# A Fourier stage folded four ways, with mirrored rows fetched and written by indirect DMAs

## The chip, the cores and the metric

The kernel runs on one core of a Trainium2 chip. The metric is the device time of one execution in microseconds. All arithmetic is in float32. The engines are named as in the profile: PE is TensorE (PEld its weight loads), DVE is VectorE, ACT is ScalarE, POOL is GpSimd, SP is SyncE, which here issues DMAs.

## The reference

Block attention with a decay is computed for four batches; its output, with the heads side by side, is a matrix x of 768 rows and 512 columns for each batch. x goes through the real part of a two-dimensional Fourier transform, is added to it, normalised by rows, and sent through a two-layer perceptron with a residual.

```python
def _moe_ref(x, w_ch1, w_ch2):              # x: (4, 768, 512)
    X = np.fft.fft(x, axis=1)               # along the 768 rows
    X = np.fft.fft(X, axis=2)               # along the 512 columns
    u = x + np.real(X).astype(np.float32)
    mu = np.mean(u, axis=-1, keepdims=True)
    var = np.mean((u - mu) ** 2, axis=-1, keepdims=True)
    un = (u - mu) / np.sqrt(var + 1e-06)
    ch = np.maximum(un @ w_ch1, 0.0) @ w_ch2   # 512 -> 2048 -> 512
    return (u + ch).astype(np.float32)
```

The attention before it, for a block of 64 rows, is a masked product of queries and keys times values, plus queries times a state, with powers of a factor `lam` per head; the state is then decayed and the block's keys and values are added to it. The two perceptron weights arrive as float64.

## The kernel before

A batch has six chunks of 128 rows. For each chunk `attn_chunk` loads keys, queries and values (SP queue, L210), transposes keys and queries (L221, L226), forms the scores of eight heads (L239), multiplies them by a decay table on VectorE (L243), updates the state (L254, L258, L259), applies state and scores (L267, L271), and transposes the result back (L278). ScalarE copies it into a tile x (L280). So the attention is done in chunks of 128 rows, not 64; the tables follow.

**The folds.** The Fourier transform of real rows needs cosines and sines only, and these are even and odd. So each chunk is folded along its columns, as soon as it is there, into sums and differences of columns d and 512-d (L288, L289 on VectorE, L287 on GpSimd for the two columns without a partner). Chunks 3 to 5 are then added to and subtracted from chunks 0 to 2 by GpSimd (L292, L293), which splits the rows' transform into even and odd frequencies (`fe`, `fo`).

**The Fourier stage** is the first part of `fft_ln`. L305 transforms along the rows, four column blocks and one single column, with tables `cs` of 193 frequencies, 30 matmuls in all; ScalarE copies the results (L313, L317) and VectorE makes a reversed copy (L320), because the frequencies above half are mirrored ones. L332 then transforms along the columns: six row tiles, four matmuls of 512 columns each, with the table `dt`. VectorE adds x (L335) and takes mean and variance (L337, L338); GpSimd forms the factor (L342, L343); VectorE normalises (L347), TensorE transposes (L351), ScalarE copies (L352).

**The perceptron**, `mlp`, works on pairs of row tiles: L363 for the first layer, relu alternately on VectorE (L369) and ScalarE (L371), L377 for the second. VectorE adds u (L382), SP stores the tile (L383). Both weights are converted from float64 on the chip, in 32 pieces of 512 columns, by VectorE and ScalarE (L181 to L189), each piece after its load (L176).

A float32 matmul is two rows in the profile, a transpose is one.

**The order.** The functions are generators that give an estimated duration after each piece, and `weave` interleaves two of them by a ratio:

```python
    run(weave(front(0), part(w, NW), 0.33))
    ...
            run(weave(part(fr, 44.0), weave(part(back, FO * 1.7 - 1.0), w, 0.9), 1.0))
            run(w)
            run(weave(fr, back, 1.0))
        elif b + 1 < B:
            run(weave(front(b + 1), back, 0.9 * t_mlp / t_front))
```

So batch 0's attention and Fourier stage run beside the first weight conversions; batch 1's beside the rest and batch 0's perceptron; batches 2 and 3 each beside the perceptron of the batch before; the last perceptron alone. From this order a scheduler makes the fixed instruction order of each engine; it can move an instruction past others by its own estimates, and each engine then runs in that order. Tiles come from pools: `xp` has twelve x tiles, `fp` one of each fold tile, `pa` five PSUM banks for the front, `pm` three for the perceptron.

Of the kernel before, what the change touches and what calls it, by code (L numbers as in the profile page):

```python
# [19 lines left out]
def _consts(S, DM):  # L20

    half, nk = S // 2, S // 4 + 1
    s = np.arange(half)
    k1 = np.stack([2 * np.arange(nk), 2 * np.arange(nk) + 1])
    ang = 2.0 * np.pi * ((s[:, None, None] * k1[None]) % S) / S

    cs = np.stack([np.cos(ang), np.sin(ang)]).reshape(2, half // 128, 128, 2, nk)
    cs = cs.transpose(2, 0, 1, 3, 4)

    h = DM // 2  # L30
    d = np.arange(h)
    k2 = np.arange(DM)
    ang = 2.0 * np.pi * ((d[:, None] * k2[None]) % DM) / DM

    dt = np.concatenate([np.cos(ang), -np.sin(ang)])
    dt[h] = np.where(k2 % 2 == 0, 1.0, -1.0)
    dt = dt.reshape(DM // 128, 128, DM).transpose(1, 0, 2)


    sgn = -np.ones((128, 1))  # L40
    sgn[0] = 1.0

    def c(m):
        return np.ascontiguousarray(m).astype(np.float32)

    return dict(cs=c(cs), dt=c(dt), sgn=c(sgn))
# [3 lines left out]
def kernel(  # L50
# [21 lines left out]
    HM = DM // 2  # L72
    G = 2
# [3 lines left out]
    cn = {n: nc.inline_tensor(a, name="k_" + n) for n, a in _consts(S, DM).items()}  # L77
# [4 lines left out]
    xp = ctx.enter_context(tc.tile_pool(name="xp", bufs=2 * NC))  # L82
# [22 lines left out]
    z = const.tile([H, 2 * C], F32, name="z")  # L105
# [26 lines left out]
    flip = fp.tile([128, 128], F32, tag="fb", name="flip")  # L132
# [19 lines left out]
    cs = const.tile([128, 2, HC, 2, NK], F32, name="cs")  # L152
    dt = const.tile([128, KO, DM], F32, name="dt")
    sgn = const.tile([128, 1], F32, name="sgn")
    w1 = const.tile([128, KO, DFF], F32, name="w1")
    w2 = const.tile([128, FO, DM], F32, name="w2")
    w1v = moe_w_ch1.rearrange("(c p) f -> p c f", p=128)
# [3 lines left out]
    def load_tables(i):  # L161
        if i == 1:
            nc.sync.dma_start(cs, cn["cs"].ap())
            nc.sync.dma_start(sgn, cn["sgn"].ap())
        elif i == 2:
            nc.sync.dma_start(dt, cn["dt"].ap())
# [34 lines left out]
    xs, folds = {}, {}  # L201
# [4 lines left out]
    def attn_chunk(b, c):  # L206
# [72 lines left out]
        x = xs[b, c] = new(xp, [C, DM], "x")  # L279
        nc.scalar.copy(x, px.rearrange("p h e -> p (h e)"))  # L280


        if c == 0:
            folds[b] = (new(fp, [C, HC, DM], "fe"), new(fp, [C, HC, DM], "fo"))
        fe, fo = folds[b]
        f = fo[:, c, :] if c < HC else new(fp, [C, DM], "fb")
        nc.gpsimd.tensor_copy(f[:, 0:DM:HM], x[:, 0:DM:HM])  # L287
        nc.vector.tensor_tensor(f[:, 1:HM], x[:, 1:HM], x[:, DM - 1:HM:-1], op=ALU.add)  # L288
        nc.vector.tensor_tensor(f[:, HM + 1:DM], x[:, 1:HM], x[:, DM - 1:HM:-1], op=ALU.subtract)  # L289
        if c >= HC:  # L290
            a = fo[:, c - HC, :]
            nc.gpsimd.tensor_tensor(fe[:, c - HC, :], a, f, op=ALU.add)  # L292
            nc.gpsimd.tensor_tensor(a, a, f, op=ALU.subtract)  # L293
        yield 1.7


    uts = {}

    def fft_ln(b):
        fe, fo = folds.pop(b)  # L300

        def dft_s(ps, cols, trig):
            for n, f in enumerate((fe, fo)):
                for t in range(HC):
                    nc.tensor.matmul(ps[:, n, :], lhsT=f[:, t, cols], rhs=cs[:, trig, t, n, :],  # L305
                                     start=(t == 0), stop=(t == HC - 1))

        ys = {}
        for c in (2, 3, 0, 1):
            ps = psum_a([128, 2, NK])  # L310
            dft_s(ps, slice(128 * c, 128 * c + 128), 0 if c < 2 else 1)
            y = new(fp, [128, NK, 2], f"y{c}")
            nc.scalar.copy(y, ps.rearrange("p n m -> p m n"))  # L313
            if c == 2:
                ps1 = psum_a([1, 2, NK])
                dft_s(ps1, slice(HM, HM + 1), 0)
                nc.scalar.copy(y[0:1], ps1.rearrange("p n m -> p m n"))  # L317
            yf = y.rearrange("p m n -> p (m n)")
            yr = new(fp, [128, S // 2], f"yr{c}")
            nc.vector.tensor_scalar(yr, yf[:, S // 2:0:-1],  # L320
                                    sgn if c == 2 else (1.0 if c < 2 else -1.0), None, op0=ALU.mult)
            ys[c] = (yf, yr)
            yield 4.0 if c == 2 else 2.0

        for g in range(NG):
            mv = new(np_, [128, G, 2], "mv")
            for i in range(G):
                T = G * g + i
                rev, tt = divmod(T, HC)
                ps = psum_a([128, DM])  # L330
                for c in range(KO):
                    nc.tensor.matmul(ps, lhsT=ys[c][rev][:, 128 * tt:128 * tt + 128], rhs=dt[:, c, :],  # L332
                                     start=(c == 0), stop=(c == KO - 1))
                u = xs[b, T]
                nc.vector.tensor_tensor(u, ps, u, op=ALU.add)  # L335
                stt = new(np_, [128, 6], "stt")
                nc.vector.bn_stats(stt, u)  # L337
                nc.vector.bn_aggr(mv[:, i, :], stt)  # L338
                yield 3.4
            ve = new(np_, [128, G], "ve")  # L340
            rs = new(np_, [128, G], "rs")
            nc.gpsimd.tensor_scalar(ve, mv[:, :, 1], EPS, None, op0=ALU.add)  # L342
            nc.gpsimd.tensor_tensor(rs, ve, mhalf, op=ALU.pow)  # L343
            ut = uts[b, g] = new(np_, [128, KO, G * 128], "ut")
            for i in range(G):
                un = new(np_, [128, DM], "un", bufs=1)
                nc.vector.tensor_scalar(un, xs[b, G * g + i], mv[:, i, 0:1], rs[:, i:i + 1],  # L347
                                        op0=ALU.subtract, op1=ALU.mult)
                pt = psum_a([128, KO, 128])
                for c in range(KO):  # L350
                    nc.tensor.transpose(pt[:, c, :], un[:, 128 * c:128 * c + 128], ident)  # L351
                nc.scalar.copy(ut[:, :, 128 * i:128 * i + 128], pt)  # L352
                yield 0.3


    def mlp(b):
        for g in range(NG):
# [15 lines left out]
            for i in range(G):  # L373
# [8 lines left out]
                nc.vector.tensor_tensor(u, ps, u, op=ALU.add)  # L382
                nc.sync.dma_start(out[b, 128 * T:128 * T + 128, :], u)  # L383
# [3 lines left out]
    def front(b):  # L387
        for c in range(NC):
            yield from attn_chunk(b, c)
        yield from fft_ln(b)  # L390
# [27 lines left out]
    run(weave(front(0), part(w, NW), 0.33))  # L418
    t_mlp = NG * (FO * 1.7 + G * 4 * 3.4)
    t_front = 66.0  # L420
    for b in range(B):
        back = mlp(b)
        if b == 0:
            fr = front(1)

            run(weave(part(fr, 44.0), weave(part(back, FO * 1.7 - 1.0), w, 0.9), 1.0))
            run(w)
            run(weave(fr, back, 1.0))
        elif b + 1 < B:
            run(weave(front(b + 1), back, 0.9 * t_mlp / t_front))  # L430
# [31 lines left out]
```

## Time and profile before

| | us |
|---|---|
| median of 3 runs (993.15 to 993.63) | 993.17 |
| the profiled execution | 996.47 |
| its span, first to last instruction | 994.5 |
| PE busy | 946.6 (95%) |
| DVE, ACT, POOL busy | 277.7, 174.9, 94.9 |
| L363 and L377, perceptron matmuls | 348.1 and 340.0 |
| L332, Fourier along columns | 44.7 + 43.0 |
| L305, Fourier along rows | 24.2 + 23.4 |
| PE idle up to the last L278 of batch 0, at 80.6 us | 32.3 |

The profiled execution is one run: durations of instructions come from it, and its span is 2.0 us shorter than its own time. In a row of the groups, the first numbers are tile names, shapes and count, then busy time and mean ns of one, then the engine's idle time ahead of it and what ended that. In a timeline a row is start, duration, engine, line and operation, with the idle time before it in brackets. Matmul rows overlap, so the step from one start to the next tells more of their cost than the duration. The clock is the share of full speed that TensorE was granted.

### The profile page before, as it was taken

The page shows a single profiled execution, that of the slowest core. Times are in us where ns is not written, and L with a number is a line of the kernel's source. Part 1 is how long each engine was busy: PE and PEld are TensorE (multiplying, and loading weights), DVE is VectorE, ACT ScalarE, POOL GpSimd, SP SyncE. Part 2 cuts the span into 40 slices and gives each one's busy share as a digit, 9 for nine tenths or more (in the row PEclk, how much of TensorE's full clock was granted, in tenths as well). Part 3 has the DMA queues.
Part 4 walks back from the last instruction along what each step waited for, and adds up shares of the span by engine and source line. Part 5 has one row for each costly group of instructions (what it writes and reads, how often), then busy time and mean ns, then how long its engine had stood idle before and what let it go on. Part 6 is the DMA issues. An engine that isn't in the chain of part 4 may idle for free.

```text
span 994.5 us, 10680 instructions
## 1 busy us (share of the span) xinstructions
PE 946.6 (95%) x4532; PEld 629.1 (63%) x4532; DVE 277.7 (28%) x546; ACT 174.9 (18%) x335; POOL 94.9 (10%) x117
## 2 busy tenths in 40 slices
PE   5569798999999999999999999999999999999998
PEld 3456476754756658568567558658657647566673
DVE  5787499522200012112102122212101212000010
ACT  4563266300000101111010002111101000000000
POOL 1223033400000001101200000011110000000000
PEclk9879999999999999999999999999999999999999
DMA  9963056300000011211100002120000000000000
GB/s 262 252 175 112 8 172 179 88 1 11 11 11 11 1 43 32 51 45 33 43 11 1 1 21 54 32 54 11 1 22 1 1 11 11 11 11 1 21 1 21
DMA packets 85039, 45.64 MB, mean 46 GB/s; under 512 B 76025, under 2 KB 77569, under 8 KB 84737
## 3 DMA queue, kind: packets, MB, share of 16 engines
q1 hardware_dynamic: 84992, 44.98, 16.5%
q8 instruction: 35, 0.57, 0.2%
q14 instruction: 12, 0.09, 0.0%
HBM read 38.67 MB, written 6.30 MB: 45 GB/s over the span
## 4 chain that ended last, share of the span: by engine, by line
PE 87%; DVE 5%; ACT 3%; POOL 1%; issue 1%; DMA 0%; POOLq 0%; DVEq 0%; ACTq 0%
PE pm L377 33%; PE pm L363 32%; PE pa L332 8%; PE pa L305 3%; PE pa L239 2%; PE pa L271 2%; PE pa L267 2%; PE pa L351 1%; PE pa L254 1%; PE pa L278 1%; ACT pw L182 1%; DVE pw L184 1%; PE pa L226 1%; PE pa L221 1%; DVE pw L181 1%
## 5 line engine op out<-in xcount | busy, mean ns | idle before, releaser
L363 PE MATMUL pm<-ut,w 128*128 128x256 f32 x1536 | 348.1, 382 | 1.2 <-ACT hr L371 1.2
L377 PE MATMUL pm<-w,hr 128*128 128x512 f32 x768 | 340.0, 594 | 0.0
L363 PEld LDWEIGHTS pm<-ut,w 128*128 128x128 f32 x1536 | 286.9, 190 | 48.1 <-issue 9.1
L377 PEld LDWEIGHTS pm<-w,hr 128*128 128x128 f32 x768 | 143.3, 190 | 165.4 <-issue 164.5
L371 ACT ACTIVATE hr<-pm 128x256 f32<-128x256 f32 x96 | 36.9, 384 | 427.2 <-PE pm L363 426.1
L369 DVE TENSOR_SCALAR hr<-pm 128x256 f32<-128x256 f32 x96 | 40.7, 424 | 238.9 <-PE pm L363 238.7
L382 DVE TENSOR_TENSOR x<-pm,x 128x512 f32<-128x512 f32 x24 | 16.6, 691 | 159.3 <-PE pm L377 159.0
L217 POOL TENSOR_TENSOR kd<-k,decay 128x512 f32<-128x512 f32 x20 | 22.5, 1126 | 254.4 <-PE pa L254 148.4
L335 DVE TENSOR_TENSOR x<-pa,x 128x512 f32<-128x512 f32 x24 | 16.6, 691 | 107.5 <-PE pa L332 107.5
L239 PE MATMUL pa<-qT,kT 64*128 64x128 f32 x384 | 32.4, 316 | 13.6 <-ACT qT L228 13.6
L332 PE MATMUL pa<-dt,y 128*128 128x512 f32 x96 | 44.7, 611 | 0.0
L239 PEld LDWEIGHTS pa<-qT,kT 64*128 64x128 f32 x384 | 27.3, 215 | 25.0 <-ACT qT L228 18.5
L332 PE MATMUL pa<-dt,yr 128*128 128x512 f32 x96 | 43.0, 592 | 0.0
L243 DVE TENSOR_TENSOR sc<-pa,decay 128x512 f32<-128x512 f32 x48 | 31.0, 685 | 22.1 <-PE pa L239 20.4
L271 PE MATMUL pa<-sc,v 128*64 128x128 f32 x384 | 30.3, 294 | 3.4 <-DVE sc L243 3.4
L332 PEld LDWEIGHTS pa<-dt,yr 128*128 128x128 f32 x96 | 17.9, 190 | 21.0 <-issue 21.0
L332 PEld LDWEIGHTS pa<-dt,y 128*128 128x128 f32 x96 | 18.3, 197 | 19.6 <-issue 18.3
L342 POOL TENSOR_SCALAR ve<-mv 128x2 f32<-128x2 f32 x12 | 3.0, 249 | 285.8 <-DVE mv L338 285.8
L271 PEld LDWEIGHTS pa<-sc,v 128*64 128x64 f32 x384 | 23.4, 146 | 9.7 <-DVE sc L243 4.6
L274 ACT COPY oT<-pa 128x512 f32<-128x512 f32 x24 | 14.0, 584 | 82.5 <-PE pa L271 82.5
L182 ACT ACTIVATE pw<-pw,cvt 128x512 uint16<-128x512 uint16 x32 | 22.9, 720 | 21.1 <-DVE pw L181 20.9
L223 ACT COPY kT<-pa 128x512 f32<-128x512 f32 x24 | 14.0, 584 | 69.8 <-PE pa L221 69.7
(65 smaller groups left out, 627.7 us busy)
## 6 DMA issues: line engine op xcount, KB each, us to landing
raw<-in_moe_w_ch_dram SPq DMA_DIRECT2D x32, 512.0 KB, 4.0
k<-in_k_dram SPq DMA_DIRECT2D x24, 256.0 KB, 3.2
q<-in_q_dram SPq DMA_DIRECT2D x24, 256.0 KB, 3.9
v<-in_v_dram SPq DMA_DIRECT2D x24, 256.0 KB, 3.0
out_dram<-x SPq DMA_DIRECT2D x24, 256.0 KB, 2.0
cs<-k_cs SPq DMA_DIRECT2D x1, 1158.0 KB, 6.4
dt<-k_dt SPq DMA_DIRECT2D x1, 1024.0 KB, 6.9
shifted<-zd SPq DMA_DIRECT2D x1, 512.0 KB, 5.7
```

The lines of the kernel that those rows point to most:

```text
L182: nc.scalar.activation(pw, pw, AF.Relu, bias=cvt[:, 0:1], scale=-1.0)
L217: nc.gpsimd.tensor_tensor(kd, kt, kpow, op=ALU.mult)
L239: mm(pss[hi][:, hp, :], lhsT=kT[HD[hi], hp, :], rhs=qT[HD[hi], hp, :], start=True, stop=True)
L243: nc.vector.tensor_tensor(t, pss[hi], decay[:, hi::2, :], op=ALU.mult)
L267: mm(po[HD[hi], hp, :], lhsT=s_old[HD[hi], hp, :], rhs=qs[HD[hi], hp, :], start=(hp == 0), stop=False, skip_group_check=True)
L271: mm(po[HD[hi], hp, :], lhsT=vt[:, 2 * hp + hi, :], rhs=sc[hi][:, hp, :], start=(c == 0 and hp == 0), stop=(hp == HP - 1), skip_group_chec ...
L305: nc.tensor.matmul(ps[:, n, :], lhsT=f[:, t, cols], rhs=cs[:, trig, t, n, :], start=(t == 0), stop=(t == HC - 1))
L332: nc.tensor.matmul(ps, lhsT=ys[c][rev][:, 128 * tt:128 * tt + 128], rhs=dt[:, c, :], start=(c == 0), stop=(c == KO - 1))
L363: nc.tensor.matmul(ps, lhsT=w1[:, c, 128 * fc:128 * fc + 128], rhs=ut[:, c, :], start=(c == 0), stop=(c == KO - 1))
L369: nc.vector.tensor_scalar(t, ps, 0.0, None, op0=ALU.max)
L371: nc.scalar.activation(t, ps, AF.Relu)
L377: nc.tensor.matmul(ps, lhsT=hr[fc // 4][:, fc % 4, 128 * i:128 * i + 128], rhs=w2[:, fc, :], start=(fc == 0), stop=(fc == FO - 1))
```

## The change

The Fourier stage now uses a second symmetry along each axis. The rows are folded as four quarters: row p goes with rows 384-p, 384+p and 768-p, and the columns likewise with 256-d and so on. The mirrored rows lie in other partitions, so each chunk of x is also stored in a DRAM tile (L320, on the ACT queue), and once all six are there five indirect DMAs on the POOL queue gather them reversed (`mirror`, L339 and L342). `fold` then makes the folded tiles for two row blocks, of 128 and of 65 rows, even parts on VectorE (L358, L359, L362, L368, L369, L375, L376) and odd parts on GpSimd (L360, L361, L364, L371, L372, L378, L379). It replaces the fold of each chunk as it comes.

L395 transforms along the rows with 20 matmuls of 193 columns. `width` transforms along the columns (L406 to L411): five matmuls of 128 or 129 columns for each of three row tiles, and three for a single row. Only half of the outputs are computed: a sum and a difference (L429, L430) give row k and its mirror 768-k, added to x on VectorE (L432) and to the gathered x on GpSimd (L433). L439 to L442 set the one row that is its own mirror. Row tiles 3 to 5 hold mirrored rows and columns; the columns are put right at the normalisation (L461) and at the output (L497, L498), the rows by an indirect DMA that scatters them to their places (L502, POOL queue) in place of a plain store by SP.

The order changes too. Batch 0's attention is woven with 12 weight pieces. Batch 0's Fourier stage then has half of batch 1's attention and four pieces beside it, and the perceptron of batch 0 starts beside the other half. The pool `xp` has ten tiles, and three more are in a new pool `xn`; the tables `cs` and `dt` are smaller, a table `ix` holds row numbers, and the five transformed tiles `ys` are fixed, zeroed once by GpSimd.

The core of the diff:

```diff
+        nc.scalar.copy(x[:, 0:HM], px[:, 0:HM])
+        nc.scalar.copy(x[:, HM:DM], px[:, DM - 1:HM - 1:-1])
...
+        nc.scalar.dma_start(xd[b][rows], x)
-        nc.vector.tensor_tensor(f[:, 1:HM], x[:, 1:HM], x[:, DM - 1:HM:-1], op=ALU.add)
-        nc.vector.tensor_tensor(f[:, HM + 1:DM], x[:, 1:HM], x[:, DM - 1:HM:-1], op=ALU.subtract)
-        if c >= HC:
-            a = fo[:, c - HC, :]
-            nc.gpsimd.tensor_tensor(fe[:, c - HC, :], a, f, op=ALU.add)
-            nc.gpsimd.tensor_tensor(a, a, f, op=ALU.subtract)
...
+    def mirror(b):
+        d = xd[b]
+        gather = nc.gpsimd.indirect_dma_start
+        r1 = [new(fp, [128, DM], f"r{a}") for a in range(2)]
+        for a, n in enumerate(BLK):
+            gather(out=r1[a][0:n], out_offset=None, in_=d[:, :], in_offset=row_of(a, n))
+        for t in range(HC):
+            u = xs[b, HC + t] = new(xp, [128, DM], "x")
+            gather(out=u[:, :], out_offset=None, in_=d[:, :], in_offset=row_of(2 + t))
...
+    def fold(b, r1):
+        for a, n in enumerate(BLK):
+            x0, x2, x3 = xs[b, a][0:n], xn_[b, HC + a][0:n], xs[b, HC + a][0:n]
+            x1 = r1[a][0:n]
...
+            V.tensor_tensor(e[0:n, 0, 0:DM], x0, x3, op=ALU.add)
+            V.tensor_tensor(e[0:n, 1, 0:DM], x1, x2, op=ALU.add)
+            P.tensor_tensor(o[0:n, 0, 0:DM], x0, x3, op=ALU.subtract)
+            P.tensor_tensor(o[0:n, 1, 0:DM], x1, x2, op=ALU.subtract)
+            V.tensor_tensor(e[0:n, :, 1:HM], e[0:n, :, 1:HM], e[0:n, :, HM:DM - 1], op=ALU.add)
+            P.tensor_tensor(o[0:n, :, 1:HM], o[0:n, :, 1:HM], o[0:n, :, HM:DM - 1], op=ALU.subtract)
...
+            V.tensor_tensor(am[:, 0, 0:HM + 1], lo, hi, op=ALU.add)
+            V.tensor_tensor(am[:, 1, 0:HM + 1], lo, hi, op=ALU.subtract)
+            P.tensor_tensor(bm[:, 0, 1:HM], lo, hi, op=ALU.subtract)
+            P.tensor_tensor(bm[:, 1, 1:HM], lo, hi, op=ALU.add)
...
+            V.tensor_tensor(f[0:n, 0], lo, hi, op=ALU.add)
+            V.tensor_tensor(f[0:n, 1], lo, hi, op=ALU.subtract)
+            P.tensor_tensor(f[0:n, 2], lo, hi, op=ALU.subtract)
+            P.tensor_tensor(f[0:n, 3], lo, hi, op=ALU.add)
...
+        for i in range(5):
+            for n in range(2):
+                for a, rows in enumerate(BLK):
+                    nc.tensor.matmul(ps[0:m, n, :], lhsT=f, rhs=cs[0:rows, a, i in (2, 3), n, :],
+                                     start=(a == 0), stop=(a == 1))
...
+        def width(t, ps, only_a):
+            mm(ps[:, HM + QM:DM], lhsT=y[2], rhs=dt[:, 2, 0:QM], start=True, stop=True)
+            mm(ps[:, HM:HM + QM + 1], lhsT=y[0], rhs=dt[:, 0, :], start=True, stop=False)
+            mm(ps[:, HM:HM + QM + 1], lhsT=y[4], rhs=dt[:, 4, :], start=False, stop=True)
+            mm(ps[:, 0:QM], lhsT=y[1], rhs=dt[:, 1, 0:QM], start=True, stop=True)
+            mm(ps[:, QM:HM], lhsT=y[3], rhs=dt[:, 3, 0:QM], start=True, stop=True)
...
+            nc.vector.tensor_tensor(even_odd(ds[:, 0:HM]), A, even_odd(B[:, :]), op=ALU.subtract)
+            nc.vector.tensor_tensor(even_odd(ds[:, HM + 1:2 * HM + 1]), A, even_odd(B[:, :]), op=ALU.add)
+            nc.vector.tensor_tensor(halves(u), halves(u), halves(ds)[:, :, 0:HM], op=ALU.add)
+            nc.gpsimd.tensor_tensor(halves(v_), halves(v_), halves(ds[:, 1:DM + 1])[:, ::-1, :], op=ALU.add)
...
-                for c in range(KO):
-                    nc.tensor.matmul(ps, lhsT=ys[c][rev][:, 128 * tt:128 * tt + 128], rhs=dt[:, c, :],
-                                     start=(c == 0), stop=(c == KO - 1))
...
+                if T < HC:
+                    nc.sync.dma_start(out[b, 128 * T:128 * T + 128, :], y)
+                else:
+                    nc.gpsimd.indirect_dma_start(out=out.rearrange("b s d -> (b s) d"),
+                                                 out_offset=row_of(2 + HC * (b + 1) + T - HC),
+                                                 in_=y[:, :], in_offset=None)
...
-    run(weave(front(0), part(w, NW), 0.33))
+    run(weave(attn(0), part(w, 0.75 * NW), 0.75 * NW / t_att))
+    fr = front(1)
+    run(weave(fft_ln(0), weave(part(fr, 0.5 * t_att), part(w, 0.25 * NW), 0.5 * NW / t_att), 1.5))
```

## The prediction

> **What bounds the kernel now.** I read the busy shares first, then the slices, the chain of waits, the costliest groups, and at last windows and timelines of single stages.
>
> ```profile
> PE 946.6 (95%) x4532; PEld 629.1 (63%) x4532; DVE 277.7 (28%) x546; ACT 174.9 (18%) x335; POOL 94.9 (10%) x117
> ...
> PE   5569798999999999999999999999999999999998
> ...
> PEclk9879999999999999999999999999999999999999
> ...
> PE 87%; DVE 5%; ACT 3%; POOL 1%; issue 1%; DMA 0%; POOLq 0%; DVEq 0%; ACTq 0%
> ...
> L332 PE MATMUL pa<-dt,y 128*128 128x512 f32 x96 | 44.7, 611 | 0.0
> ...
> L332 PE MATMUL pa<-dt,yr 128*128 128x512 f32 x96 | 43.0, 592 | 0.0
> ```
>
> TensorE is busy 95% of the span, and its idle time lies in the first eight slices; after that every matmul that is dropped is time gained, if nothing makes TensorE wait. Here is TensorE by stages (us, busy and rows, clock, DMA share, GB/s); the cuts are the last L278 of batch 0, its first L332, its last L351, and batch 1's last L278:
>
> ```profile
> 0.00:80.60 80.60, 48.26 (x424) 0.85 0.80 217
> 80.60:93.00 12.40, 11.52 (x65) 1.00 0.64 191
> 93.00:133.20 40.20, 34.52 (x114) 0.96 0.12 40
> 133.20:187.40 54.20, 50.40 (x463) 1.00 0.57 157
> 187.40:199.40 12.00, 11.22 (x85) 1.00 0.38 84
> 199.40:994.50 795.10, 790.63 (x3390) 1.00 0.07 18
> ```
>
> From 133.2 on, 852.2 us are busy and 9.1 idle (3.6 of them the tail): 133.2 + 852.2 + 9.1 = 994.5. Batch 2's turn from attention to Fourier shows how the present folds hide (timeline of TensorE):
>
> ```profile
> 719.22 0.60 PE L278 MATMUL pa<-ident,oT 128*128 128x128 f32 x4
> 719.66 7.03 PE L377 MATMUL pm<-w,hr 128*128 128x512 f32 x16
> 726.52 1.14 PE L305 MATMUL pa<-cs,fe 128*128 128x193 f32 x6
> ```
>
> Copy, fold and GpSimd adds fit under 6.87 us of L377. The last view is the one that the forecast hangs on, VectorE and GpSimd side by side:
>
> ```profile
> 83.68 0.68 DVE L184 SCALAR_TENSOR_TENSOR pw<-raw,pw 128x512 uint16<-128x512 uint16 x1
> 83.91 1.58 POOL L292 TENSOR_TENSOR fe<-fo,fb 128x512 f32<-128x512 f32 x1 [1.03 <-DVE fb L289]
> 84.28 1.48 DVE L181 TENSOR_SCALAR pw<-raw 128x512 uint16<-128x512 uint16 x1
> ...
> 85.56 1.33 POOL L293 TENSOR_TENSOR fo<-fo,fb 128x512 f32<-128x512 f32 x1
> 85.69 1.75 DVE L189 SCALAR_TENSOR_TENSOR w<-w,pw 128x512 f32<-128x512 f32 x1
> ```
>
> L181 usually takes 0.42 and L189 0.68; each here ends only when the GpSimd add ends, and L292 (1.27 at least) grows to 1.58. They take turns.
>
> **What the Trainium skill says.** "SBUF — State Buffer", Who interferes with whom: a VectorE instruction with two SBUF inputs and a GpSimd instruction that reads SBUF exclude each other for the whole instruction; the lines above agree. "GPSIMD Engine Reference", 4.1 Engine selection: two-input elementwise work is about 2x slower there; the trace agrees (128x512: 1.27 against 0.69). "TensorE: Matmul & The Clock Gate", What's actually happening: after an idle window of some 3.4 us TensorE runs at half clock, and some 3.4 us of work restore it; agrees: four L221 take 0.86 at 23.95 and 0.44 when busy. "DMA: Bandwidth & Descriptors", Anatomy of one DMA: a DMA issued by GpSimd takes 2.0 us plus bytes/436e3, 2.6 for 256 KB; Latency: about 1 us of it until the first byte. No run here shows one.
>
> **The change part by part.**
>
> *Removed from TensorE.* The width stage (L332) has 24 matmuls of 512 columns a batch, 21.6 us; now 15 of 128 or 129 columns and three one-row ones. L305 starts an instruction of 193 columns each 0.163 us, so 128 columns take 0.108; L278's 128x128 step is 0.11 (719.22 to 719.66 for four), so loading does not bind. Two instructions a matmul: 18 x 0.22 = 4.0. If loads of 190 ns (PEld rows of L332) did not overlap: 18 x 0.38 = 6.8. I take 4.0. The sequence stage (L305) falls from 30 matmuls to 20, 0.327 each: 9.8 to 6.5. Together 20.9 us a batch, **84 in all** (72 with the dear price).
>
> *Added ahead of the first Fourier matmul, in each batch.* The last chunk's x is copied in two pieces (ACT, two of about 0.38), stored to DRAM (2.0, as the outputs land), fetched mirrored by five gathers on POOL, and folded by 14 VectorE and 14 GpSimd instructions over two row blocks (65 rows cost as much as 128). VectorE: per block three of 0.60 and four of 0.34 (L188's and L289's starts), 3.2. GpSimd: three of 1.27 and four of 0.64 (L292; L258's 0.62), 6.4. By the turns shown above these add: 2 x 9.6 = 19.2. A gather's hold on POOL is between 1.0 (first byte) and 2.6 (whole transfer, one after another); I take 1.3, the lower end plus the 0.3 by which L292 is stretched, and 1.8 while weight conversion fills VectorE. All these gathers, and a 1.3 us scatter of the output, stand in POOL's in-order queue before or between the folds.
>
> *Batches 2 and 3.* From the last transpose: copies until 1.4, store landed and seen 3.6, five gathers until 10.1, the third landed 9.5. Taking turns, VectorE has the even half of block 0 at 14.8 (9.5 + 2.6 of folds + 2.7 of GpSimd's turns), GpSimd the odd half at 19.8 (10.1 + 6.4 + scatter 1.3 + 2 of VectorE's), that of block 1 at 27.6 (10.1 + 12.8 + 1.3 + 3.4). TensorE's built order there is 16 L377 (6.9), 9 MLP-up matmuls (3.9), two even Fourier ones, one odd, two MLP-up, then block 1: it waits 3.6, 4.3 and 6.6 us, 14.5, and 1.5 for the clock: **16 a batch, 32**. Bounds: 13 (gather 1.0), 23 (2.6).
>
> *Batch 1.* POOL issues three gathers; the fourth waits for a buffer (`xp` has 10) until output tile 0 of batch 0 is added, the fifth for tile 1. First wait: conversion shares VectorE and ACT (stored 5.5, third gather 10.9, landed 12.7; folds 2.6, conversion 1.3, turns 4.8), even data at 21.4, cover 20 MLP-up matmuls (9.1): 12.3. Second: tile 0 added, gather 1.3 + landing 1.8, 4.5 of odd folds plus turns of 2.5, about 11, against 7 L377 (6.0): 5. Then 3 in small waits up to the normalised transposes, 2 for the clock: **22** (15 to 31). Before, this stretch (187.4 on) idled 0.8.
>
> *Batch 0.* Of 13 weight conversions ahead of the last scores 10 are left in the built order, and the folds of 0.68 a chunk go: 3 x 2.5 + 4 = 11 us of VectorE, of which I count two thirds: last L278 at 73 for 80.6 (67 to 79). Store landed 5.5 after, five gathers of 1.8 until 14.5, GpSimd's folds 12.8 with 7 of VectorE's turns until 34, the last odd matmuls and chunk 0 of batch 1 until 40 (93.0 - 80.6 = 12.4 before). Then widths, normalisation and chunks 1 and 2: 17 of VectorE rows in a chain (adds and `bn_stats` of 0.60, quarters of 0.34) and some 10 of hand-overs: 27.5. Last transposes at 73 + 40 + 27.5 = **140.5** (129 to 153), with 15.2 us of batch 1's attention done (5.1 a chunk, 5.1 us being its warm rows in the chain) and 5.6 less of L363.
>
> *The other edits.* Copies in halves, `un` in halves, `y` in halves, the x0 fix-ups: VectorE and ACT gain under 5 us a batch, under MLP matmuls that leave VectorE 80% idle. Stores (1.5 MB) and gathers replace 1.4 MB of smaller tables in the loaded first 75 us: nothing. Last scatter instead of L383: 1.4 more at the tail.
>
> *The sum.* 140.5, plus TensorE's rest 852.2 - 15.2 + 5.6 - 3 x 20.9 = 779.9, plus waits: attention of batch 1 beside conversion 5 (5.3 before), batch 1 22, batches 2 and 3 32, tail 5. Total 984.4 us of span against 994.5: **10 us less**. The profiled execution took 996.47 in all, 3.3 above the median of 993.17; the same difference from the median gives **983**.
>
> **Rivals.**
> (a) *More of the gain stays.* Gathers of 1.0 and folds that overlap freely: batch 0 -10, batch 1 -5, the others -5 each, 25 less: 958. For it: POOL is busy 10%. Against: the turns at 84 us.
> (b) *The POOL queue becomes the bound; slower.* Gathers and scatters at 2.6: batch 0 +4 (5 x 0.8), batch 1 +4, batches 2 and 3 six each by 1.3, +16: 24 more, 1007. It decides where a hold is about 0.5 us over my prices, since 20 of them stand on the path and 10 us are to be lost. For it: L258 took 3.82 us once and a two-element L287 4.06 in dense VectorE stretches, six times normal. Against: their medians stay at 0.62 and 0.44.
> (c) *Everything is hidden:* 993 - 84 = 909. Against: the order above puts at most 12 us of matmuls over 27 of chain. The order also shows that the matmuls do go, so "nothing changes" is only a balance of gain and waits, 991 to 995.
>
> **How the numbers follow.** Forecast (965 to 991) 0.42; (a) with (c) 0.18; balance 0.10; (b) 0.30. A difference under 0.2%, 2 us, is about what a measurement of this kernel can tell from none. Signs are mixed; the likeliest case alone spans 965 to 991, and the range of 953 to 1010 leaves 0.2 outside, with (c) and the far end of (b). Faster 0.60, same 0.10, slower 0.30.
>
> **What would show it.** TensorE busy near 865 us; L406 to L411 together near 16 us. Waits of L395 on POOL and DVE folds of 11 to 20 us in each later batch, and clock digits under 9 there. Gathers and scatters as POOL work of 1.3 us; GpSimd folds stretched beside VectorE's. Batch 0's last L465 near 140. It is wrong if L395 waits little (then 950), if TensorE's small matmuls cost their loads (12 more), or if POOL's holds exceed 1.8 us.

## The result and the profile after

The changed kernel takes 1003.25 us (median of 4 runs, 999.76 to 1007.08), the one before on the same chip 993.16: a ratio of 1.0105, 95% interval 1.0059 to 1.0152. **It is slower by 1%.** The forecast was 983 and faster. The profiled execution took 1007.08, its span is 1005.3. It is the slowest of the four: they differ by 7 us, and their granted clocks with them (0.937, 0.940, 0.947, 0.947).

From the page of the changed kernel, the lines that answer to those of before: busy shares, slices, granted clock, chain.

```profile
PE 892.6 (89%) x4404; PEld 616.0 (61%) x4404; DVE 323.7 (32%) x610; ACT 186.1 (19%) x411; POOL 165.7 (16%) x176
...
PE   4642989598899999999986999999986999999997
...
PEclk9985799786999999999996999999995999999999
...
PE 73%; POOL 6%; DVE 6%; issue 3%; DMA 3%; ACT 1%; POOLq 0%; ACTq 0%
```

TensorE's busy time fell by 54.0 us, its idle time (span less busy) rose from 47.9 to 112.7. The clock, 0.986 of full speed over the span before, is 0.937. Its low digits stand beside or just after the idle ones: in batch 0's Fourier stage (slices 3 to 5), in batch 1's (8 to 10), in batch 2's (22) and in batch 3's (31). POOL and DVE, 1% and 5% of the chain before, now have 6% each.

By stages (us, busy and count for PE, PEld, DVE, ACT, POOL, then clock, DMA share, GB/s). The cuts: the last L313 of batch 0, its first L395, its last L465, batch 1's last L313, batch 1's last L465.

```profile
0.00:64.90 64.90, 38.33 (x428) 28.90 (x428) 52.39 (x101) 38.28 (x68) 13.99 (x26) 1.00 0.97 254
64.90:92.06 27.16, 0.11 (x2) 0.03 (x1) 18.97 (x22) 6.82 (x13) 16.65 (x15) 0.58 0.40 108
92.06:144.90 52.84, 45.02 (x336) 37.21 (x336) 31.19 (x61) 16.66 (x42) 19.88 (x20) 0.76 0.36 102
144.90:182.00 37.10, 32.09 (x272) 25.53 (x272) 34.89 (x71) 26.05 (x46) 3.12 (x3) 0.95 0.71 199
182.00:270.50 88.50, 69.88 (x229) 44.64 (x228) 45.05 (x81) 18.22 (x43) 30.04 (x28) 0.81 0.13 43
270.50:1005.30 734.80, 707.19 (x3144) 479.70 (x3144) 141.17 (x278) 80.05 (x200) 82.05 (x85) 0.97 0.09 27
```

Batch 0's Fourier stage begins with 27 us in which TensorE does nothing, and goes on at a clock of 0.76; batch 1's (182 to 270.5) has 18.6 us of idle and a clock of 0.81. Before, the last 795 us of the run went at 1.00.

Batch 2's turn from attention to Fourier, where the kernel before went from L377 straight into L305 (timeline of TensorE, changed kernel):

```profile
512.97 0.60 PE L313 MATMUL pa<-ident,oT 128*128 128x128 f32 x4
513.41 7.03 PE L491 MATMUL pm<-w,hr 128*128 128x512 f32 x16
520.28 4.05 PE L477 MATMUL pm<-ut,w 128*128 128x256 f32 x18
530.71 2.52 PE L395 MATMUL pa<-cs,fs 128*128 128x193 f32 x6 [6.39 <-DVE fs L375]
533.03 1.91 PE L477 MATMUL pm<-ut,w 128*128 128x256 f32 x4
539.76 2.30 PE L395 MATMUL pa<-cs,fs 65*128 65x193 f32 x6 [4.82 <-POOL fs L378]
```

Two waits, 6.4 and 4.8 us, in brackets. What the reader should see beside them is the work between and after: four L477 rows take 1.91, while 18 at full clock took 4.05. They run at half speed. VectorE and GpSimd in the same stretch (timeline of these two):

```profile
523.04 3.42 DVE L358 TENSOR_TENSOR fe<-x,x 128x512 f32<-128x512 f32 x1 [1.06 <-DMA x<-xd,ix]
523.40 1.28 POOL L361 TENSOR_TENSOR fo<-r,xn 128x512 f32<-128x512 f32 x1
524.63 1.27 POOL L360 TENSOR_TENSOR fo<-x,x 128x512 f32<-128x512 f32 x1
...
527.37 1.27 POOL L364 TENSOR_TENSOR fo<-fo 128x510 f32<-128x510 f32 x1
527.44 1.49 DVE L368 TENSOR_TENSOR fe<-fe 128x257 f32<-128x257 f32 x1 [0.26 <-ACT fe L363]
```

L358, which needs 0.60, holds VectorE for 3.42: it ends only when two GpSimd folds are through.

### The profile page after: what moved, and what is told of

The parts are those of the page before. It is cut to its first block, busy times and chain, and to the rows that moved or that the text cites. A ratio compares the mean times of both kernels' runs of the same rounds, so it can differ in the third digit from the quotient of the medians.

```text
span 1005.3 us, 10721 instructions
## 1 busy us (share of the span) xinstructions
PE 892.6 (89%) x4404; PEld 616.0 (61%) x4404; DVE 323.7 (32%) x610; ACT 186.1 (19%) x411; POOL 165.7 (16%) x176
## 3 DMA queue, kind: packets, MB, share of 16 engines
q1 hardware_dynamic: 83264, 40.73, 15.5%
## 4 chain that ended last, share of the span: by engine, by line
PE 73%; POOL 6%; DVE 6%; issue 3%; DMA 3%; ACT 1%; POOLq 0%; ACTq 0%
PE pm L477 30%; PE pm L491 29%; PE pa L395 4%; PE pa L306 2%; PE pa L274 2%; DMA x<-xd,ix 1%; PE pa L302 1%; PE pa L465 1%; PE pa L313 1%; PE pa L289 1%; POOL fo L360 1%; POOL fo L364 1%; POOL r L339 1%; DVE pw L219 1%; PE pa L261 1%
## 5 line engine op out<-in xcount | busy, mean ns | idle before, releaser
L477 PE MATMUL pm<-ut,w 128*128 128x256 f32 x1536 | 356.9, 389 | 1.7 <-DVE hr L483 0.7
L477 PEld LDWEIGHTS pm<-ut,w 128*128 128x128 f32 x1536 | 293.3, 194 | 47.7 <-issue 5.4
L395 PE MATMUL pa<-cs,fs 65*128 65x193 f32 (+1 forms) x128 | 42.7, 509 | 63.8 <-DVE fs L375 49.6
L497 DVE TENSOR_TENSOR y<-pm,x 128x256 f32<-128x256 f32 x24 | 10.2, 424 | 218.6 <-PE pm L491 218.6
L395 PEld LDWEIGHTS pa<-cs,fs 65*128 65x128 f32 (+1 forms) x128 | 36.2, 309 | 70.1 <-issue 39.4
L502 POOL DMA_INDIRECT out_dram<-y,ix x12 | 12.5, 1043 | 325.2 <-DVE y L498 324.9
L274 PE MATMUL pa<-qT,kT 64*128 64x128 f32 x384 | 30.5, 298 | 11.4 <-ACT qT L263 11.4
L278 DVE TENSOR_TENSOR sc<-pa,decay 128x512 f32<-128x512 f32 x48 | 31.3, 684 | 22.0 <-PE pa L274 20.3
L266 DVE TENSOR_TENSOR qs<-pa,qpow 128x512 f32<-128x512 f32 x20 | 13.8, 689 | 64.5 <-ACT qT L263 64.5
L433 POOL TENSOR_TENSOR x<-x,ds 128x512 f32<-128x512 f32 x12 | 18.2, 1515 | 77.3 <-DVE ds L430 70.4
L339 POOL DMA_INDIRECT r<-xd,ix x8 | 8.6, 1079 | 129.4 <-DMA xd<-xn 128.2
```

What stands on the lines that cost most here:

```text
L274: mm(pss[hi][:, hp, :], lhsT=kT[HD[hi], hp, :], rhs=qT[HD[hi], hp, :], start=True, stop=True)
L278: nc.vector.tensor_tensor(t, pss[hi], decay[:, hi::2, :], op=ALU.mult)
L339: gather(out=r1[a][0:n], out_offset=None, in_=d[:, :], in_offset=row_of(a, n))
L395: nc.tensor.matmul(ps[0:m, n, :], lhsT=f, rhs=cs[0:rows, a, i in (2, 3), n, :], start=(a == 0), stop=(a == 1))
L433: nc.gpsimd.tensor_tensor(halves(v_), halves(v_), halves(ds[:, 1:DM + 1])[:, ::-1, :], op=ALU.add)
L477: nc.tensor.matmul(ps, lhsT=w1[:, c, 128 * fc:128 * fc + 128], rhs=ut[:, c, :], start=(c == 0), stop=(c == KO - 1))
```

## The experiments

Theory W: waits for the chain of store, gathers and folds, with the half clock after them, take more than the matmuls give. Rivals: M, the many small matmuls cost more than the few wide ones; P, the turns of VectorE and GpSimd; Q, the queue of gathers; O, the new order of batches 0 and 1. Each kernel was timed beside executions of the kernel before; the ratio to these, with its interval, is what compares. Span, busy, idle and clock are TensorE's in the profiled execution, which lies between 3 us below and 9 us above its median (run 2 is the one at 9), so small differences between these columns tell nothing.

| kernel | median us | ratio (95%) | span | busy | idle | clock | waits of the row matmuls (L395) |
|---|---|---|---|---|---|---|---|
| before | 993.16 | 1 | 994.5 | 946.6 | 47.9 | 0.986 | 1.7 (L305) |
| changed | 1003.25 | 1.0105 (1.0059 to 1.0152) | 1005.3 | 892.6 | 112.7 | 0.937 | 63.7 |
| 1 cover in batches 2, 3 | 968.45 | 0.9735 (0.9695 to 0.9775) | 964.3 | 875.7 | 88.6 | 0.958 | 40.7 |
| 2 cover in all batches | 969.29 | 0.972 (0.9677 to 0.9763) | 977.0 | 889.8 | 87.2 | 0.949 | 14.0 |
| 3 no folds | 907.93 | 0.9111 (0.9076 to 0.9146) | 905.4 | 856.2 | 49.2 | 0.998 | none |
| 4 all folds on VectorE | 950.0 | 0.9543 (0.9508 to 0.9578) | 945.4 | 867.8 | 77.6 | 0.977 | 26.0 |
| 5 three gathers early | 990.3 | 0.9957 (0.9943 to 0.9971) | 986.8 | 886.0 | 100.8 | 0.953 | 49.2 |
| 6 order as before | 1015.1 | 1.0227 (1.0194 to 1.0259) | 1011.7 | 896.9 | 114.8 | 0.930 | 59.3 |
| 7 VectorE, gathers early | 941.51 | 0.9489 (0.9458 to 0.952) | 937.0 | 869.1 | 67.9 | 0.975 | 17.8 |
| 8 as 7, order as before | 955.84 | 0.9638 (0.9602 to 0.9674) | 952.4 | 877.3 | 75.1 | 0.963 | 20.2 |
| 9 short cover, idle wait | 996.86 | 1.0015 (0.9993 to 1.0038) | 997.4 | 890.4 | 107.0 | 0.945 | 59.0 |
| 10 wait filled, folds held | 1013.29 | 1.02 (1.0148 to 1.0253) | 1010.4 | 912.1 | 98.3 | 0.941 | 49.2 |
| 11 as 7, chunk ahead in batch 0 | 943.34 | 0.9482 (0.944 to 0.9525) | 940.2 | 872.0 | 68.2 | 0.971 | 7.8 |
| 12 wait filled | 993.89 | 1.0007 (0.9992 to 1.0023) | 991.2 | 899.9 | 91.3 | 0.964 | 41.5 |

**1, cover in batches 2 and 3.**

```diff
         sets = fold(b, r1)
+        if b >= 2:
+            yield 13.0
...
-    t_att, t_front = NC * 7.3, NC * 7.3 + 17.0
+    t_att, t_front = NC * 7.3, NC * 7.3 + 30.0
```

> In batches 2 and 3 the lead generator reports 13 units of its time after the folds, so that 28 MLP-down and 8 MLP-up matmuls (about 27 us) stand between the last attention transpose and the first Fourier matmul, where 8 and 9 (about 11 us) stood. Theory W (waits for the store-gather-fold chain, and the half clock after them, eat the gain): batch 2 has 11.2 us of idle and about 4 us of half clock, batch 3 10.5 and about 7; nearly all of it goes, 1003 becomes 970 to 980. Theory M (the many small matmuls cost more than the few wide ones did, whatever stands before them): no change, 1000 to 1006. Theory P (GpSimd and VectorE turns stretch every stage): 995 to 1003, since the folds are the same.

3.7% below the changed kernel (0.9735/1.0105), two lines of scheduling and nothing else. Busy falls by 16.9 with the same 4404 matmul rows, idle by 24.1. The two waits of each of these batches, 21.7 us, are gone, and with them their half clock, 11.2 us (how it is counted stands under run 3); the small rest lies in batches 0 and 1, which the edit leaves alone. That is W's number, even a little under it; neither M nor P, as the whole explanation, allows for it.

**2, cover in all batches.** The report is 13 units, 36 in batch 1.

> The same cover in all four batches: in batch 0 two and a half chunks of batch 1's attention are put ahead of the first Fourier matmul, in batch 1 the report is 36 units. Theory W: beyond the run with cover in batches 2 and 3 alone, batch 0 (27 us idle, about 10 us of half clock) gives 10 to 20 us and batch 1 (15 us idle, about 10 of half clock) 5 to 15, so 940 to 965. Theory O (the order of batch 1's attention beside batch 0's folds is itself the cost): batch 0 gives nothing, 965 to 980. Theory M: 1000 to 1006.

Nothing beyond run 1: the intervals overlap almost wholly. In batch 0 the wait moves (timeline of TensorE, run 2):

```profile
97.06 1.97 PE L302 MATMUL pa<-qs,st 64*64 64x128 f32 x16 [8.78 <-DVE qs L266]
...
138.18 1.09 PE L466 MATMUL pa<-ident,un 128*128 128x128 f32 x4 [8.13 <-DVE un L462]
```

The attention put ahead needs VectorE for qs and masks, where the folds and the weight conversion stand; later the normalised tiles are late (L466 there is the kernel's L465). By these waits VectorE's work, not the order of TensorE, is the limit of this stage; run 11 tries it once more. In batch 1 a wait of 9.5 us stays, since the scheduler still places three Fourier matmuls early. So W's second half missed. The 969 lies in O's range; O itself is tested by runs 6 and 8.

**3, no folds.**

```diff
+    zf = const.tile([128, 4, 2, QM], F32, name="zf")   # zeros; zq likewise
+    def fold(b, r1):
+        return [(zf, zq), (zf, zq)]
```

> Left out: all 28 fold instructions of a batch; the Fourier matmuls read a constant tile of zeros, so the result is not the reference's. Stores, gathers, scatters and all matmuls stay. It shows what the change is worth to TensorE when nothing waits for folds. Theory W: 905 to 925, TensorE busy 850 to 870 (before: 946.6). Theory M (small matmuls cost more): TensorE busy still 885 or more, time 940 or more. If the gathers themselves are the bound (the output adds read gathered tiles): 930 to 960 with waits at the normalised transposes.

Page of run 3, busy line and clock:

```profile
PE 856.2 (95%) x4404; PEld 589.9 (65%) x4404; DVE 260.9 (29%) x554; ACT 181.7 (20%) x395; POOL 99.2 (11%) x122
...
PEclk9999999999999999999999999999999999999999
```

The same 4404 rows cost 856.2 us at clock 0.998 and 892.6 in the changed kernel. **36.4 us of the changed kernel's busy time are half clock.** Run 3 multiplies zeros, which might matter by itself, but the changed kernel's own trace says the same: its busy time in windows of 0.5 us, each times what the granted clock lacks of 1.00, adds up to 37.1 us. By batches this is 10.8 in the Fourier stage of batch 0 and 1.4 just after it, 13.8 in batch 1, 4.1 in batch 2 and 7.1 in batch 3. In the kernel before it is 10.4, all in the first 133 us. M is out, and so is the idea that the gathers bound the output adds.

**4, all folds on VectorE.**

```diff
-            V, P = nc.vector, nc.gpsimd
+            V, P = nc.vector, nc.vector
```

> All 28 folds of a batch on VectorE, none on GpSimd. Alone, a fold of 512 takes VectorE 0.60 and one of 256 0.34, so a batch's folds take 12.8 us where the two engines by turns took 16 to 17 (from 523 to 540 in batch 2). Theory P: even data of block 0 some 3 us earlier, odd data of block 1 some 5 us earlier, 3 to 5 us less in each of four batches: 985 to 993. Theory W without P (only the distance counts, turns do not): 1000 to 1004. If GpSimd's help is worth more than the turns: slower, 1006 to 1015.

About four times the gain that P expected: 5.6% below the changed kernel (0.9543/1.0105). Timeline of VectorE and TensorE, run 4, batch 2 (its last L313 starts at 481.57):

```profile
491.74 0.69 DVE L358 TENSOR_TENSOR fe<-x,x 128x512 f32<-128x512 f32 x1 [0.58 <-DMA x<-xd,ix]
492.35 0.69 DVE L360 TENSOR_TENSOR fo<-x,x 128x512 f32<-128x512 f32 x1
492.95 0.68 DVE L362 TENSOR_TENSOR fe<-fe 128x510 f32<-128x510 f32 x1
493.55 0.68 DVE L364 TENSOR_TENSOR fo<-fo 128x510 f32<-128x510 f32 x1
...
495.97 1.60 PE L395 MATMUL pa<-cs,fs 128*128 128x193 f32 x8 [1.75 <-DVE fs L375]
```

From the last L313 the even data of block 0 take 14.4 us instead of 17.7, the last fold 21.6 instead of 27.6. I had put a few us on each wait. But the first wait in batch 2 falls from 6.4 to 1.75, the second vanishes, and with both goes the half clock; in batch 0 the first L395 comes 10 us earlier. The scheduler also put 12 L477 matmuls ahead of the first L395 instead of 9, 1.3 us; so not all of it is the folds. Busy falls by 24.8, idle by 35.1. The run also leaves open how much of the gain is the turns: GpSimd is slower by itself, and by the prediction's prices its half of the folds takes 12.8 us a batch undisturbed, as long as all of them take VectorE. In batch 2 of the changed kernel GpSimd's folds took 15.5 us, with a scatter of 1.3 between them. No run has GpSimd's folds without the turns.

**5, three gathers early.**

```diff
+            xe[b] = dram.tile([S // 3 * 2 + 1, DM], F32, name=f"xe{b}")
+        if c < 4:
+            nc.scalar.dma_start(xe[b][rows], x)
+        elif c == 4:
+            nc.scalar.dma_start(xe[b][512:513], x[0:1])
...
             yield from attn_chunk(b, c)
+            if c == NC - 2:
+                early(b)      # both r tiles and the mirrored tile 2, from xe
```

> Three of a batch's five gathers (both r tiles and the mirrored tile of output tile 2) read a second table in DRAM that holds rows 0 to 512 and is complete one chunk earlier, so that they and the folds of x1 with x2 of both blocks no longer follow the last chunk's store; the chunks 0 to 3 and one row of chunk 4 are stored twice. Folds stay split over VectorE and GpSimd. Theory Q (the queue of five gathers and the folds behind it are the chain): from the last transpose to the even data of block 0 13 to 14 us instead of 17.7, to the odd data of block 1 about 21 instead of 27.6; 6 to 10 us less in each batch with its half clock, 965 to 985. Theory T (only the turns of the two engines matter, gathers are hidden): 998 to 1005.

Faster than the changed kernel by 1.5% (0.9957/1.0105), between Q and T. In batch 2 (timeline of TensorE; the last L313 starts at 499.68, and the L404 of this kernel is L395):

```profile
512.51 2.52 PE L404 MATMUL pa<-cs,fs 128*128 128x193 f32 x6 [3.20 <-DVE fs L384]
522.66 2.30 PE L404 MATMUL pa<-cs,fs 65*128 65x193 f32 x6 [5.07 <-POOL fs L387]
```

The even data of block 0 come 12.8 us after the L313, as Q says; the last fold of block 1 ends at 23.8, where the changed kernel had 27.6 and Q about 21. Two waits stay, and 5.4 us of half clock in each of batches 2 and 3. The gathers are part of the chain, the smaller part.

**6 and 8, the order of batches 0 and 1 as before.**

```diff
+    run(weave(front(0), part(w, NW), 0.33))
...
+            fr = front(1)
+            run(weave(part(fr, 44.0), weave(part(back, FO * 1.7 - 1.0), w, 0.9), 1.0))
-    run(weave(fft_ln(0), weave(part(fr, 0.5 * t_att), part(w, 0.25 * NW), 0.5 * NW / t_att), 1.5))
```

> The changed folds and widths with the order of batches 0 and 1 as it was before: batch 1's attention begins only after batch 0's Fourier stage, weights are converted under the whole of batch 0's front. Theory O (the new order costs): faster than the changed kernel, 985 to 998. Theory W (waits for the folds cost, and attention of batch 1 fills some of them): slower, since batch 0's first Fourier matmul then waits about 27 us with nothing beside it and the 15 us of attention come later beside weight conversion, 1005 to 1020.

> As the run before it, with the order of batches 0 and 1 of the kernel before. Theory O: faster than that, by 5 to 15 us. Theory W: slower by 3 to 15 us, as batch 0's fold chain is then covered by nothing.

Slower by 1.2% (1.0227/1.0105) in the changed kernel, by 1.6% (0.9638/0.9489) in the fastest. O is out: the new order is worth 12 and 14 us, which fits the attention of batch 1 that it lays under batch 0's folds.

**7, VectorE and early gathers**, both edits together.

> All folds on VectorE and three gathers early. The run with folds on VectorE alone (950) still had 17.0 us of wait ahead of the Fourier stage of batch 0, about 9 in batch 1 and 1.8 in each of batches 2 and 3. Theory Q: the wait of batch 0 falls to 10 to 13, the others go: 930 to 940. Theory T: the gathers are hidden already, 946 to 952.

Between the two theories, nearer to Q: 0.9489 of the kernel before, where all folds on VectorE alone gave 0.9543 (the two intervals overlap at their edges). With run 11 it is the fastest of all, and some 5% faster than the kernel before. The wait of batch 0 is still 14.7.

**11, one chunk of batch 1 ahead in batch 0:** run 7 with `yield 6.0` after batch 0's folds.

> All folds on VectorE, three gathers early, and the generator of batch 0 reports 6 units after its folds, so that one chunk of batch 1's attention stands ahead of batch 0's first Fourier matmul. The run without it (941.5) waits 14.7 us there. Theory W: the chunk fills 5 to 8 of these, 933 to 938. If VectorE, which does the folds, the conversion and the chunk's masks, sets the end of this stage: no gain, 940 to 946.

Waits of the row matmuls fall to 7.8, and nothing is gained, as the second case has it: the waits for `un`, which VectorE makes, grow from 6.2 to 11.4 us, as in run 2.

**9, 10 and 12: is the half clock a cost of its own?** Run 9 has a little more cover (`yield 4.0` between `mirror` and `fold` in batches 2 and 3). Runs 10 and 12 add useless matmuls to it that are due where TensorE waits; nobody reads what they write.

```diff
+            if b >= 2:
+                pw_ = psum_m([128, DM])
+                for j in range(7):      # run 10: 5, with rhs = e[0:n, 0, 0:DM]
+                    nc.tensor.matmul(pw_, lhsT=w2[:, 0, 0:128], rhs=xs[b, HC + a], start=True, stop=True)
```

> Partner of the next run. In batches 2 and 3 the generator reports 4 units between the gathers and the folds, so 12 MLP-up matmuls instead of 9 stand after the 8 MLP-down ones (12.1 us of cover, even data of block 0 due at 17.7), and TensorE stands idle in what is left. Theory C (the half clock after a wait is a cost of its own): a wait of 4 to 5 us and another of 3 to 5 in each batch, each followed by clock 0.5; PE busy about 890; 990 to 1002. Without C: PE busy near 880.

> The run before it, and in batches 2 and 3 five added matmuls of 512 columns for each of the two row blocks, which read a half-done fold and write a bank that nobody reads: 4.3 us of useless work twice in a batch, 17.4 in all, laid where TensorE waits for the rest of the fold. Theory C: the clock stays up in these stages, so TensorE's busy time rises by only 6 to 10 us for 17.4 us of added work, idle falls by 10 to 14, and the whole is 2 to 8 us faster than its partner although it does more. Without C: busy rises by the full 17.4 and the whole is 3 to 8 us slower, since not all of the added work fits the waits.

> Mends the run with filled waits, where the added matmuls read a half-done fold that the next fold overwrites, and so held the folds up. Here 14 added matmuls of 512 columns a batch (12.2 us at full clock, 24.4 in batches 2 and 3 together) read the gathered tiles, which the folds do not overwrite, and stand behind the same 12 MLP-up matmuls as in the run with idle waits (996.9 us, 1.0015 of the kernel before; it waits 5.2 and 3.9 us in batch 2, and its matmuls between and after these waits take 4.7 us more than at full clock). Theory C: 12.2 us of useless work take the place of 9.1 us of idle and 4.7 of half clock, so that it costs nothing: 993 to 999, ratio 0.998 to 1.004, TensorE busy up by 15 to 17 for 24.4 of added work. Without C: busy up by 24, 1000 to 1006, ratio 1.006 to 1.012.

Run 9 is as expected; in batch 2 it has these two waits (timeline of TensorE, run 9, whose L397 is L395):

```profile
528.41 1.01 PE L397 MATMUL pa<-cs,fs 128*128 128x193 f32 x2 [5.20 <-DVE fs L375]
...
536.87 2.30 PE L397 MATMUL pa<-cs,fs 65*128 65x193 f32 x6 [3.92 <-DVE fs L375]
```

Run 10 failed as a test: the added matmuls read a half-done fold, the next fold overwrites it, and so had to wait for them; the wait that was to be filled stayed. But its timeline of TensorE, and one window of it, show the clock bare:

```profile
519.07 4.53 PE L363 MATMUL pm<-fe,w 128*128 128x512 f32 x10 [0.92 <-DVE fe L358]
528.89 3.59 PE L401 MATMUL pa<-cs,fs 128*128 128x193 f32 x8 [5.29 <-DVE fs L379]
532.27 8.74 PE L363 MATMUL pm<-fe,w 65*128 65x512 f32 x10
...
532.20:540.80 8.60, 8.60 (x11) 3.44 (x11) 0.00 (x0) 0.00 (x0) 0.34 (x1) 0.50 0.01 2
```

Ten rows of 512 columns take 4.53 us before the wait of 5.29, and 8.74 after it, at a clock of 0.50. Run 12 reads tiles that no fold overwrites, and fills the wait (windows of run 12 in batch 2):

```profile
505.00:518.00 13.00, 13.00 (x46) 8.08 (x45) 3.59 (x4) 1.03 (x3) 6.76 (x7) 1.00 0.37 109
518.00:531.00 13.00, 12.75 (x32) 5.63 (x31) 12.32 (x12) 0.87 (x4) 12.41 (x12) 1.00 0.06 24
531.00:533.00 2.00, 1.32 (x8) 1.05 (x7) 1.73 (x3) 0.19 (x1) 1.92 (x3) 1.00 0.00 0
533.00:540.00 7.00, 7.00 (x37) 6.32 (x36) 0.69 (x2) 1.40 (x3) 0.35 (x1) 1.00 0.00 0
```

The clock stays at 1.00. From the last L313 of batch 2 to its first width matmul, with the same other work between, run 12 takes 50.1 us with its 14 added matmuls and run 9 takes 50.7 without; in batch 3 it is 49.4 against 50.3. In the whole kernel 28 useless matmuls, 24.4 us at full speed, cost nothing: 1.0007 against 1.0015, intervals overlapping. Busy rises by 9.5, not 24.4, even less than theory C expected: 9.3 us of half clock in batches 2 and 3 are gone, and 4.4 in the first 65 us, where the two kernels are the same, so that this part is chance. So the half clock is a cost of its own, and it is caused by the waits.

## Why the prediction was wrong

**The ledger.** Span is busy plus idle. Of the 946.6 us busy before, 10.4 were half clock, so 936.2 were work at full clock; of the 892.6 now, 36.4 are half clock and 856.2 work. Against the kernel before that is 80.0 us less work, 26.0 more for half clock, 64.8 more idle; together 10.8 more, 994.5 to 1005.3. The forecast had busy near 865 and a span of 984.4, so 119 us for idle and clock, 5 of it clock (2 in batch 1, 1.5 each in batches 2 and 3, and no term for it in batch 0). Measured are 112.7 of idle and 36.4 of half clock. **The step that failed is the price of the half clock:** 31 us too low, where the whole miss of the span is 20.9. Idle was priced too dear by 1.7 and work at full clock by 8.8, which hid part of it. The 8.8 are not the matmuls but the attention of batch 0: the same work (424 and 428 rows) took 48.26 us at clock 0.85 before and 38.33 at 1.00 now, and the forecast had left that busy time as it was. This was partly luck, since runs 1 and 9, the same up to there, lose 3.1 and 4.4 us to half clock in their first 65 us, and run 12 nothing.

**Matmuls removed: nearly right.** 84 us were forecast and some 80 came. Groups of the changed kernel, by shape:

```profile
L395 PE MATMUL pa<-cs,fs 128*128 128x193 f32 x64 | 25.9, 522 | 49.6 <-DVE fs L375 49.6
L395 PE MATMUL pa<-cs,fs 65*128 65x193 f32 x64 | 24.1, 497 | 14.1 <-POOL fs L378 14.1
L406 PE MATMUL pa<-dt,ys 128*128 128x128 f32 x24 | 5.7, 321 | 0.0
```

A row of L395 lasts 0.52 where L305's took 0.33. In run 4 the same groups are 17.2 and 14.7, so some 18 of the 50 us are half clock. L406 to L411 are 30.9 and not 16 in the groups, and still 27.9 in run 3 at full clock, because the groups count overlapping rows in full. From start to start the five matmuls of a row tile take 1.12 us in batch 2 (554.96 to 556.08), which is the 0.22 a matmul of the forecast; that sign was set on the wrong measure.

**Batches 2 and 3: the chain right, its price not.** From the last transpose of batch 2 I had the store seen at 3.6, the gathers done at 10.1, odd block 0 at 19.8 and odd block 1 at 27.6; the trace has 4.2, 10.4, 19.2 and 27.6. Only even block 0 was off, 17.7 for 14.8: I let VectorE and GpSimd take turns one by one, and L358 waited for two. Waits of 14.5 were forecast; 11.2 and 10.5 came. The clock, counted at 1.5, cost 4.0 in batch 2 and 7.0 in batch 3, from rows before and after the waits set against like rows at full clock (20 L395 rows in batch 3: 6.64, in run 4: 3.71). Windows of the changed kernel, batch 3 and then batch 1, each after its second wait:

```profile
765.80:768.70 2.90, 2.90 (x8) 2.77 (x9) 0.23 (x1) 0.56 (x2) 0.82 (x1) 0.50 0.00 0
768.70:772.00 3.30, 3.30 (x12) 3.25 (x11) 0.00 (x0) 0.40 (x2) 0.00 (x0) 0.50 0.00 0
772.00:775.20 3.20, 3.20 (x12) 3.20 (x11) 0.00 (x0) 1.00 (x2) 0.00 (x0) 0.50 0.00 0
...
234.70:240.00 5.30, 5.25 (x16) 5.25 (x17) 0.28 (x1) 0.50 (x1) 0.86 (x1) 0.50 0.00 0
240.00:244.70 4.70, 4.70 (x15) 2.93 (x14) 0.00 (x0) 1.50 (x3) 0.00 (x0) 0.50 0.00 0
244.70:248.00 3.30, 3.30 (x13) 2.37 (x12) 0.00 (x0) 0.50 (x1) 0.00 (x0) 0.50 0.00 0
```

The Trainium skill ("TensorE: Matmul & The Clock Gate", What's actually happening) has about 3.4 us of work for the return to full clock; I read 1.5 us of loss out of it, and once per batch. Here, after the second wait, some 4 us of work passed at half clock in batch 2, but some 10 in batch 3 and 15 in batch 1 (234.75 to about 250), and 14 in run 10 (528.9 to about 543), most of them dense matmuls of 512 columns. The measurement decides. Why it varies these runs don't show; the waits of batches 2 and 3 were much the same (6.4 and 5.7, then 4.8 twice).

**Batch 1.** Waits of 12.3, 5 and 3 were forecast; 10.5, 4.5 and 3.5 (0.25, 0.9 and 2.3) came. The second one hangs on a buffer, as forecast: the gather at 225.31 stood 22.5 us behind L498, an output add of batch 0. (The forecast's "about 11" for it is a sum of 10.1.) The clock was put at 2 and cost 13.8. The stretch from its first row of block 1 to the start of the second width tile's last matmul takes 15.8 (234.75 to 250.5); the same rows take 8.6 in run 4 (211.10 to 219.7): 7 us for the second wait alone.

**Batch 0.** Its last transposes came at 144.9 for 140.5, inside the bounds, by two errors that cancel in part. Attention ended at 64.9, not 73, and so before the early end of my bounds. VectorE was busy 8.7 us less up to there (61.04 to 52.39; 11 counted, two thirds of it credited), and the clock stayed up, for which I had no term; what each is worth these runs don't show. From there the folds took 35 us (34 forecast), but the last row matmuls were done after 52 (40 forecast). Some 7 of these 12 us are half clock, in which TensorE ran from 92 to about 113 us (an estimate from busy time and clock); the rest is work after the folds that I had counted too short.

**The gathers.** A hold on POOL is 1.0 us, but 0.3 passes before the next, so the pace of 1.3 was right: in batch 2 five gathers took 6.2 us for 6.5. A gather lands 3.3 to 3.4 after its hold begins, where I had 3.1 to 3.3. The queue is no bound at these prices, so rival (b), whose number of 1007 comes close, had the wrong mechanism, and its closeness is luck: the kernel is slower with cheap holds. That only 10 us were there to lose, as (b) says, was right, but the clock lost them. Attention of batch 1 beside conversion: 5.0 of idle, 5 forecast. Tail: 5.9 for 5.

**Where the choice lay.** The signs were in the profile before: clock digits under 9 beside the early waits, and 48.26 us of busy time at a clock of 0.85 before the last L278 of batch 0. A wait of 5 us on TensorE should have been priced at 5 plus the work it slows.

## What to carry to other kernels

Price a wait on TensorE twice: the idle time, and the loss of the work that follows at half clock, which here was between a third and three quarters of a batch's waits again. Useless matmuls in such a wait were free in run 12; in run 10, where the awaited folds had to wait for them, they cost nearly 2%. A chain split between VectorE and GpSimd need not be shorter: from the landing of a batch's third gather to its last fold, all on VectorE took 11.5 us, split over both 17.5. Their turns and GpSimd's slower pace (1.27 against 0.60 for 512 columns) both have a part in this, and the runs don't say how much. Before giving up on a change that removes work, move what it waits for: two edits turned a loss of 1% into a gain of 5% here.

## What the runs showed of the hardware

The Trainium skill ("SBUF — State Buffer", Who interferes with whom) has the exclusion for a single instruction; that VectorE's 0.60 us instruction took 3.42 us behind two GpSimd instructions in a row (523.04, and 3.46 at 79.72) I had not expected. Of the prediction's two stretched VectorE lines only L189 has the two inputs that it names; L181 reads one tile. In run 4, with GpSimd out of the folds, no fold of batch 2 takes over 0.69. An indirect DMA of 128 rows of 2 KB held GpSimd for 0.99 us on average and landed 3.4 us after issue; the store of as many bytes on ScalarE's queue took 2.1 and 2.7, the medians of its two groups. Not every wait cost clock: those of 1.75 and 1.58 us in batches 2 and 3 of run 4 left it at 1.00.
